# Moving the start of two loads in a decode attention kernel: x waits for GpSimd's last constant, the first K load waits for the x transposes

## The chip, the cores and the metric

The kernel runs on one core of one Trainium2 chip. The metric is the device time of one execution in microseconds (us). All runs quoted here are of one core. The kernel before repeats within 0.5 us.

## The reference

Two independent attention blocks, A and B, decode one token each for 8 sequences. Each has 32 heads of width 128 and a cache of 4096 keys and values per head, all in bf16.

```python
# for A and for B: x (8,1,1024), k_cache and v_cache (8,32,4096,128), wq (1024,4096), wo (4096,1024)
q = (x @ wq).reshape(B, Sq, H, Dh).transpose(0, 2, 1, 3)
scores = einsum("bhqd,bhkd->bhqk", q, k_cache) * (Dh ** -0.5)
p = softmax(scores, axis=-1)
o = einsum("bhqk,bhkd->bhqd", p, v_cache)
a = o.transpose(0, 2, 1, 3).reshape(B, Sq, H * Dh) @ wo
# result: concatenate([a, b], axis=-1)
```

The caches are large and each element is used once, so nearly all of the kernel's traffic is K and V: the profile counts 1107 MB read.

## The kernel before

All big loads go through a ring of three slots of 64 KB per partition, 8 MiB each. SyncE issues them in the order of a plan: A_wq, the first K load, B_wq, the second K load, then V and K in turns, last the two wo. Each load waits until the former tenant of its slot has been used. Two small loads (16 KB each) bring x to the third slot, which B_wq takes over once TensorE has transposed x.

```python
plan = [("wq", 0, 1), ("k", 0, 0), ("wq", 1, 2)]          # (what, which, slot)
for n in range(NQ - 1):
    plan.append(("k", n + 1, (n + 1) % 2))
    plan.append(("v", n, 2))
# ...
def load_tiles():
    while issued[0] < len(plan):
        kind, n, w = plan[issued[0]]
        prev = before[issued[0]]                              # former tenant of the slot
        dep = c_oh if (kind, n) == ("k", 0) else opUse.get(prev)
        if prev is not None and dep is None:
            return
        # ... dma(to, from_, ("t", w), [dep]) on SyncE

# GpSimd writes constants, one after another: ident, own_m, PM, E; c_E is the last of them.
c_oh = add("dve", lambda e: e.tensor_copy(own_h[:], own), [c_own])    # a VectorE constant

x_sb = ring[0:NC * B, 2, 0:D]
op_x = [dma(x_sb[c * B:(c + 1) * B, :], caches[c][0].rearrange("b s d -> b (s d)"), ("x", 0), [c_oh], "act") for c in range(NC)]
def emit_xT(e): ...                                           # 8 TensorE transposes of x
op_xT = opUse[("x", 0)] = add("pe", emit_xT, [c_ident, op_x[-1]])
load_tiles()
c_xT = add("dve", lambda e: e.tensor_copy(xT[:], misc_bf16[:, 0:NC * DC * B]), [op_xT])
make_q(0)                                                     # needs A_wq and xT
# ... make_qT, make_stage, make_qbc; then 64 steps of multiply, fold, reduce, softmax, PV
```

`add(engine, instruction, waits)` and `dma(out, in, semaphore, waits, engine)` record operations; a wait becomes a semaphore wait only where it is needed. A_wq has no wait and is issued first.

Of the kernel before, what the change touches and what calls it, by code (L numbers as in the profile page):

```python
# [31 lines left out]
class _Program:  # L32
# [11 lines left out]
    def add(self, eng, emit, deps=(), dma_key=None, moves=False):  # L44
        op = _Op(eng, emit, list(deps), dma_key, moves)
        if dma_key is not None:
            self.counts[dma_key] = self.counts.get(dma_key, 0) + 16
            op.token = (dma_key, self.counts[dma_key])
        for d in op.deps:
            if not (d.eng == "pe" and eng == "pe"):  # L50
                d.sig = True
        self.ops[eng].append(op)
        return op
# [86 lines left out]
def _build_kernel(nc, caches, out):  # L140
    B, Sq, D = caches[0][0].shape
    _, H, Sk, Dh = caches[0][1].shape
    NC = len(caches)
# [18 lines left out]
    with es:  # L162
# [44 lines left out]
        def dma(out_ap, in_ap, key, deps, eng="sp"):  # L207
            return add(eng, lambda e: e.dma_start(out_ap, in_ap), deps, dma_key=key)


        def pool_select(view, base, pattern, dep, op=ALU.not_equal, fill=1.0, step=1):
            return add("pool", lambda e: e.affine_select(out=view, in_=view, compare_op=op, fill=fill,
                                                         base=base, pattern=pattern, channel_multiplier=step), [dep])
# [9 lines left out]
        c_E = add("pool", lambda e: e.memset(E[:], 0.0))  # L223
        for q in range(4):
            c_E = pool_select(E[:, :, PH - 1:].rearrange("p i (j u) -> p i j u", u=PH)[:, :, :, 0], -32 * q, [[-8, 4], [-1, HQ]], c_E)
        c_oh = add("dve", lambda e: e.tensor_copy(own_h[:], own), [c_own])
# [5 lines left out]
        opOc, opNorm, opProj, opUse, opPM, opEv = {}, {}, {}, {}, {}, {}  # L232
# [16 lines left out]
        def where(n):  # L249

            return n // (B * HB), n // HB % B, n % HB
# [4 lines left out]
        def load_tiles():  # L256
            while issued[0] < len(plan):
                kind, n, w = plan[issued[0]]
                prev = before[issued[0]]
                dep = c_oh if (kind, n) == ("k", 0) else opUse.get(prev)  # L260
                if prev is not None and dep is None:
                    return
                to, key = ring[:, w, :], ("t", w)
                if kind in ("k", "v"):
                    c, b, hb = where(n)
                    from_ = caches[c][1 if kind == "k" else 2][b, hb * HQ:(hb + 1) * HQ].rearrange("u (m t) d -> (u m) (t d)", m=MP)
                    opT[(kind, n)] = dma(to, from_, key, [dep])
                elif kind == "wq":
                    opT[(kind, n)] = dma(to[:, 0:DC * H * Dh], caches[n][3].rearrange("(p k) n -> p (k n)", k=DC), key, [dep])
                else:  # L270
                    from_ = caches[n][4].rearrange("(p r) n -> p (r n)", r=H)
                    for i, (r0, r1) in enumerate(wo_cuts if n == NC - 1 else ((0, H),)):
                        opT[(kind, n, i)] = dma(to[:, r0 * D:r1 * D], from_[:, r0 * D:r1 * D], key if n < NC - 1 else ("w", i), [dep])
                issued[0] += 1
# [168 lines left out]


        x_sb = ring[0:NC * B, 2, 0:D]
        op_x = [dma(x_sb[c * B:(c + 1) * B, :], caches[c][0].rearrange("b s d -> b (s d)"), ("x", 0), [c_oh], "act") for c in range(NC)]

        def emit_xT(e):
            for k in range(DC):
# [2 lines left out]
            return i  # L452
# [3 lines that stand above are left out]
        make_q(0)  # L456
# [5 lines left out]
        for n in range(NQ):  # L462
            P.mark(n)
            for r in range(NR):
                s = n * NR + r
                make_mul(s)
                if s >= LAG:
                    make_red(s - LAG)
                if r == LAG - 1 and n >= 1:
                    make_shift(n - 1)  # L470
                fold = make_fold(s)
                if r == LAG - 1 and n >= 1:
                    make_pm(n - 1)
                if n == 0 and r == NR - 1:
                    for c in range(1, NC):
                        make_q(c)
                        make_qT(c)
                if r == 2 and n >= 1:
                    make_pv(n - 1, 0, RG // 2)
                if r == 3 and n >= 1:  # L480
                    make_pv(n - 1, RG // 2, RG)
                    make_acc(n - 1)
                if r == 2 and n + 1 < NQ:
                    make_stage(n + 1)
                    make_qbc(n + 1)
                make_eacc(s, fold)
                load_tiles()
                if r == 3 and n >= 1:
                    make_ext(n - 1)
        P.mark(NQ)  # L490
        n = NQ - 1
# [3 lines left out]
        make_pv(n, 0, RG)  # L495
        make_acc(n)
        load_tiles()
        make_ext(n)
        c_norm = make_norm()
# [34 lines left out]
def bass_concat_heads__mha_block_cached__mha_block_cached__decode_kernel(  # L534
    nc, A_x, A_k_cache, A_v_cache, A_wq, A_wo, B_x, B_k_cache, B_v_cache, B_wq, B_wo, out,
):
    caches = [(A_x, A_k_cache, A_v_cache, A_wq, A_wo), (B_x, B_k_cache, B_v_cache, B_wq, B_wo)]
    _build_kernel(nc, caches, out)
# [28 lines left out]
```

## Time and profile before

| | before |
|---|---|
| time, median of the first 3 runs | 2564.36 us (2564.36 to 2564.61) |
| span of the profiled execution | 2562.5 us |
| data read, mean rate | 1107 MB, 432 GB/s |
| VectorE busy | 85% |

These are lines of the page of the kernel before: its span, the rows of VectorE and of the DMA engines (busy tenths in 40 equal slices of the span), the DMA totals, and the costliest group of instructions (busy us, mean ns of one, then the engine's idle time just before them and what ended most of it).

```profile
span 2562.5 us, 18439 instructions
...
DVE  3798898898898898898898888988988988988983
...
DMA  9999999999999999999999999999999999999999
...
DMA packets 19545, 1107.49 MB, mean 432 GB/s; under 512 B 2208, under 2 KB 2240, under 8 KB 2384
...
L328 DVE TENSOR_TENSOR ring<-ring,qbc 128x8192 bf16<-128x8192 bf16 x256 | 1131.1, 4418 | 310.5 <-DMA ring<-in_A_k_cache_dram 157.3
```

The DMA row has no slice under 9. VectorE, the busiest engine of compute, still idles 310 us in all ahead of its first multiply of each K tile, and what ends that is a K load (A's 157 us, B's 153). So the DMA stream sets the pace. The single packet records say the same: a 64 KB packet takes 2.42 us on one of 16 engines, which is 65536 B x 16 / 2.42 us = 433 GB/s. This agrees with the Trainium skill, DMA: Bandwidth & Descriptors, section Where 436 GB/s comes from, which puts the ceiling of the 16 ports at 435 GB/s. Between the first data packet at 1.83 us and 2550 us the engines stand idle for 0.25 us each on average (16 minus the packets in flight, summed over time and divided by 16).

The start is the part that the change touches. This is the timeline of before there; the columns are start, duration, engine (SPq and ACTq are the queues that issue DMAs), line, operation, and in brackets how long the engine idled and what ended it.

```profile
0.80 0.40 SPq L208 DMA_DIRECT2D ring<-in_A_wq_dram  x1
...
4.20 0.35 SPq L208 DMA_DIRECT2D ring<-in_A_k_cache_dram  x1
4.21 0.59 ACTq L208 DMA_DIRECT2D ring<-in_A_x_dram  x1
...
4.30 1.49 POOL L212 TENSOR_SCALAR_AFFINE_SELECT E<-E 128x32 bf16<-128x32 bf16 x4
...
18.13 0.64 PE L450 MATMUL misc<-ident,ring 16*128 16x16 bf16 x8 [18.13 <-DMA ring<-in_B_x_dram]
18.80 0.33 SPq L208 DMA_DIRECT2D ring<-in_B_wq_dram  x1
...
22.95 3.59 PE L284 MATMUL o<-ring,xT 128*8 128x512 bf16 x32 [4.19 <-DMA ring<-in_A_wq_dram]
...
42.20 4.43 DVE L328 TENSOR_TENSOR ring<-ring,qbc 128x8192 bf16<-128x8192 bf16 x1 [8.50 <-DMA ring<-in_A_k_cache_dram]
```

A_wq, issued at 0.80, is at hand at 22.9. The first K load, issued at 4.20, is queued behind it and has landed at 42.2. The two small x loads, issued at 4.21 and 4.84, have both landed only at 18.0, because their packets take turns with those of A_wq. The packet records of one of the engines that serve x show it (start in us, duration in us, queue, bytes; q1 is SyncE's queue, q10 ScalarE's):

```
   7.221  2.420  q1   65536
   9.637  0.084  q10   2048     x of A
   9.717  2.418  q1   65536
  12.131  0.009  q10      4     its completion increment
  12.137  2.418  q1   65536
  14.551  0.084  q10   2048     x of B
  14.631  2.418  q1   65536
  17.045  0.009  q10      4     its completion increment
```

A note on clocks. The packet times in this document count from the same start as the timelines. The recorded texts below were written with packet times 0.30 us too late. The view by stretches shows it: data packets of A_wq (590 GB/s in the last column, where a packet counts at its start) start before 2.00 us already, where the recorded prediction has the first at 2.13:

```profile
1.00:2.00 1.00, 0.00 (x0) 0.00 (x0) 0.00 (x0) 0.00 (x0) 0.63 (x4) 1.00 1.74 590
```

So where a recorded text has a packet at 22.2, read 21.9, and where it takes 1.33 or 1.3 us from an issue to its first packet, read 1.03 (0.80 to 1.83). Each forecast of a turn or of a hole sets one packet time against another, so the error cancels there. Issue times, times of instructions and durations are not affected.

### The profile page before, as it was taken

The numbers are of one execution on the slowest core, as the hardware profiler recorded it, in microseconds if no ns is written. First come the engines' busy times: TensorE is split into PE (matmuls) and PEld (weight loads), VectorE is DVE, ScalarE is ACT, GpSimd is POOL, SyncE is SP. The second block draws the span as 40 slices with busy tenths as digits, with TensorE's granted clock in tenths as the row PEclk, the third lists the DMA queues.
The fourth block names the chain that finished last, engine by engine and source line by source line (L and its number), as shares of the span: only waits on it lengthen the run. The fifth ranks groups of instructions, "written<-read, shape, count | busy, mean of one in ns | idle before, by whom it ended". The sixth has DMA issues, their size and how long they took to land.

```text
span 2562.5 us, 18439 instructions
## 1 busy us (share of the span) xinstructions
PE 1120.6 (44%) x7520; PEld 391.4 (15%) x7520; DVE 2172.9 (85%) x1034; ACT 130.9 (5%) x403; POOL 4.3 (0%) x15
## 2 busy tenths in 40 slices
PE   2443443443444444434444444444444434434435
PEld 0111111111111111111111111111111111111112
DVE  3798898898898898898898888988988988988983
ACT  1100000000000000000000000000000000000000
POOL 0000000000000000000000000000000000000000
PEclk7676766766766666766666666767767676767677
DMA  9999999999999999999999999999999999999999
GB/s 425 427 438 430 437 431 437 431 437 431 437 431 437 431 437 431 437 431 435 432 436 430 436 431 437 431 435 433 432 436 432 435 431 437 431 436 432 436 432 394
DMA packets 19545, 1107.49 MB, mean 432 GB/s; under 512 B 2208, under 2 KB 2240, under 8 KB 2384
## 3 DMA queue, kind: packets, MB, share of 16 engines
q1 hardware_dynamic: 19472, 1107.32, 99.9%
q8 instruction: 6, 0.10, 0.0%
q10 hardware_dynamic: 64, 0.05, 0.0%
q14 instruction: 3, 0.02, 0.0%
HBM read 1107.33 MB, written 0.03 MB: 432 GB/s over the span
## 4 chain that ended last, share of the span: by engine, by line
DMA 51%; DVE 28%; issue 16%; PE 4%; another core or an unknown queue 0%; ACT 0%; DVEq 0%; SPq 0%; POOL 0%; POOLq 0%
DMA ring<-in_A_k_cache_dram 25%; DMA ring<-in_B_k_cache_dram 25%; DVE ring L328 10%; DVE ring L333 10%; PE red L343 4%; DVE s_sb L351 4%; DVE PM L368 3%; DMA ring<-in_B_wo_dram 2%; DVE rmax L357 1%; DVE rtmp L358 0%; ACT PM L290 0%; DVEq L135 0%; PE o L284 0%; DVE ngm L361 0%
## 5 line engine op out<-in xcount | busy, mean ns | idle before, releaser
L328 DVE TENSOR_TENSOR ring<-ring,qbc 128x8192 bf16<-128x8192 bf16 x256 | 1131.1, 4418 | 310.5 <-DMA ring<-in_A_k_cache_dram 157.3
L343 PE MATMUL red<-ring,ident 128*128 128x512 bf16 x2048 | 781.7, 551 | 1392.3 <-DVE ring L333 1392.3
L333 DVE TENSOR_TENSOR ring<-ring 128x4096 bf16<-128x4096 bf16 x256 | 581.4, 2271 | 0.0
L343 PEld LDWEIGHTS red<-ring,ident 128*128 128x128 bf16 x2048 | 238.9, 127 | 1843.5 <-DVE ring L333 1494.5
L351 DVE TENSOR_REDUCE s_sb<-red 128x64 f32<-128x1024 f32 x256 | 311.1, 1215 | 3.3 <-PE red L343 3.3
L380 PE MATMUL pv<-ring,PM 128*32 128x512 bf16 x4096 | 275.4, 416 | 4.7 <-DVE PM L368 4.7
L368 DVE TENSOR_TENSOR PM<-pe,own_h 128x2048 bf16<-128x2048 bf16 x64 | 146.1, 2284 | 0.7 <-ACT pe L363 0.7
L380 PEld LDWEIGHTS pv<-ring,PM 128*32 128x32 bf16 x4096 | 104.2, 104 | 189.3 <-issue 117.1
L317 ACT ACTIVATE qbc<-misc 128x128 bf16<-128x128 f32 x64 | 17.7, 277 | 1091.9 <-PE misc L315 1091.9
L363 ACT ACTIVATE pe<-s_sb,ngm 128x256 bf16<-128x256 f32 x64 | 32.5, 508 | 471.5 <-DVE ngm L361 471.5
L388 ACT ACTIVATE accS<-pv 128x512 bf16<-128x512 f32 x64 | 38.2, 597 | 351.8 <-PE pv L380 351.8
L397 PEld LDWEIGHTS o<-accS,E 128*32 128x32 bf16 x1024 | 31.3, 100 | 49.3 <-issue 48.1
L397 PE MATMUL o<-accS,E 128*32 128x32 bf16 x1024 | 38.1, 185 | 0.7 <-ACT accS L388 0.7
L403 ACT ACTIVATE o_sb<-o 32x32 f32 (+1 forms) x64 | 11.8, 185 | 449.7 <-PE o L397 449.7
L357 DVE TENSOR_REDUCE rmax<-s_sb 128x1 f32<-128x256 f32 x64 | 26.9, 420 | 2.2
L436 DVE CAST orow<-proj 8x512 bf16<-8x512 f32 x2 | 1.4, 679 | 24.6 <-PE proj L426 24.6
L426 PE MATMUL proj<-ring,on_sb 128*8 128x512 bf16 x128 | 16.4, 411 | 11.7 <-DMA ring<-in_A_wo_dram 8.0
L310 ACT ACTIVATE qst<-qT 128x128 bf16 (+1 forms) x64 | 18.7, 293 | 2.3 <-DVE qT L303 2.3
L358 DVE TENSOR_SCALAR rtmp<-half,rmax 128x32 f32<-128x32 f32 x64 | 15.4, 241 | 2.3
L303 DVE COPY qT<-misc 128x256 bf16<-128x256 bf16 x2 | 2.5, 1272 | 17.2 <-PE misc L299 17.2
L315 PE MATMUL misc<-ident,qst 128*128 128x128 bf16 x64 | 14.8, 232 | 1.7 <-ACT qst L310 1.7
L361 DVE TRANSPOSE_TENSOR_REDUCE ngm<-rtmp 128x1 f32<-128x32 f32 x64 | 13.5, 211 | 2.2
(34 smaller groups left out, 65.1 us busy)
## 6 DMA issues: line engine op xcount, KB each, us to landing
ring<-in_B_wo_dram SPq DMA_DIRECT2D x1, 4608.0 KB, 31.7
ring<-in_B_wo_dram SPq DMA_DIRECT2D x1, 2048.0 KB, 36.3
ring<-in_B_wo_dram SPq DMA_DIRECT2D x1, 1024.0 KB, 38.3
ring<-in_A_k_cache_dram SPq DMA_DIRECT2D x32, 39.8
ring<-in_A_v_cache_dram SPq DMA_DIRECT2D x32, 27.8
ring<-in_B_k_cache_dram SPq DMA_DIRECT2D x32, 40.0
ring<-in_B_v_cache_dram SPq DMA_DIRECT2D x32, 27.9
ring<-in_B_wo_dram SPq DMA_DIRECT2D x1, 512.0 KB, 39.1
```

Of the source, the lines that this page charges most:

```text
L310: return e.activation(qst[:, n % 2, :].rearrange("p (j m) -> p j m", m=MP), from_.unsqueeze(2).to_broadcast([128, HQ, MP]), ACTF.Copy)
L317: opQbc[n] = add("act", lambda e: e.activation(qbc[:, n % 2, :], misc[:, 0:Dh], ACTF.Copy), [opQb[n], _at(opMul, NR * (n - 2) + NR - 1)])
L328: opMul[s] = add("dve", lambda e: e.tensor_tensor(v, v, qbc[:, n % 2, :].unsqueeze(1).to_broadcast([128, CT, Dh]), ALU.mult), [opT[("k", n ...
L333: return add("dve", lambda e: e.tensor_tensor(v[:, :, 0:64], v[:, :, 0:64], v[:, :, 64:128], ALU.add), [opMul[s]])
L343: i = e.matmul(dst, ident[:], v[:, g, :, j, :], start=(j == 0), stop=(j == 3))
L351: opRed[s] = add("dve", lambda e: e.tensor_reduce(s_sb[:, n % 2, r * CT:(r + 1) * CT], red_ps[s % 2][:, :].rearrange("p (t w) -> p t w", w ...
L357: m = add("dve", lambda e: e.tensor_reduce(rmax[:], s_sb[:, n % 2, :], AX.X, ALU.max), [opRed[NR * n + NR - 1]])
L363: opExp[n] = add("act", lambda e, at: e.activation(pe[:], s_sb[:, n % 2, :], ACTF.Exp, bias=ngm[:, n % 2:n % 2 + 1], scale=scale, accum_ou ...
L368: opPM[n] = add("dve", lambda e: e.tensor_tensor(PM[:], pe[:].unsqueeze(2).to_broadcast([128, T, HQ]), own_h[:].unsqueeze(1).to_broadcast( ...
L380: i = e.matmul(pv_ps[32 * q:32 * (q + 1), :], PM[:, t:t + 4, :].rearrange("p t j -> p (t j)"), v[:, t * Dh:(t + 4) * Dh], start=(g == 0), ...
L388: opAcc[n] = add("act", lambda e: e.activation(accS[:], pv_ps[:], ACTF.Copy), [opPV[n], _at(opExt, n - 1)])
L397: x = e.matmul(to, E[:, i, PH - 1 - u:PH - 1 - u + MB], accS[:, i * 128 + H * u:i * 128 + H * (u + 1)], start=(i == 0 and u == 0), stop=(i ...
```

## The change

Its intent: the x loads and the first K load stay out of the way until A_wq's descriptors have been generated, so that the first weight load is generated alone. Only two waits change.

```diff
-                dep = c_oh if (kind, n) == ("k", 0) else opUse.get(prev)
+                dep = op_xT if (kind, n) == ("k", 0) else opUse.get(prev)
...
-        op_x = [dma(..., ("x", 0), [c_oh], "act") for c in range(NC)]
+        op_x = [dma(..., ("x", 0), [c_E], "act") for c in range(NC)]
```

The order of instructions on every engine stays the same.

More of the change, by code (lines that the diff above doesn't have):

```diff
@@ L445, in _build_kernel @@
         x_sb = ring[0:NC * B, 2, 0:D]
-        op_x = [dma(x_sb[c * B:(c + 1) * B, :], caches[c][0].rearrange("b s d -> b (s d)"), ("x", 0), [c_oh], "act") for c in range(NC)]
+        op_x = [dma(x_sb[c * B:(c + 1) * B, :], caches[c][0].rearrange("b s d -> b (s d)"), ("x", 0), [c_E], "act") for c in range(NC)]
         def emit_xT(e):
```

## The prediction

> **What bounds it.** The core's DMA engines. The page's DMA row reads 9 in all 40 slices and its byte line 1107 MB at 432 GB/s over 2562.5 us; VectorE is 85% busy and, by the groups, waits for K loads. The packet records of the trace agree: almost every packet is 64 KB, 2.42 us each; on 16 engines such packets alone take 2539 us. Their mean idle time between the first data packet (2.13 us) and 2550 us is 0.25 us. So only the 2.1 us before the first packet, a hole in the DMA stream, and the last 10 us can change the time.
>
> **What the change does.** Only waits move; instructions and their order stay. The first weight load (A_wq) is issued at 0.80 us as before. Timeline of before: the first K load is issued at 4.20, the x loads at 4.21 and 4.84, both released by VectorE's constant; the x packets land by 18, the transposes run 18.13 to 18.77, B_wq is issued at 18.80; A_wq has landed at 22.9, the first K load at 42.2.
> - The x loads now wait for GpSimd's last select (4.30 + 1.49 = 5.79): issued at about 5.8 instead of 4.2.
> - The first K load goes from 4.2 to about 18.8, right before B_wq, in the same order of the queue. A_wq occupies all 16 engines until about 22.2, so a K load issued at 18.8 still queues behind data.
>
> **What is critical.** The x loads are slow because each of their packets takes turns with a 64 KB packet of A_wq (first x packets at 9.94, then 12.4, 14.9, 17.3). This is the turn by turn arbitration per packet of the Trainium skill, DMA: Bandwidth & Descriptors, section Queues, rings and completion order; the trace's alternation agrees. From issue to first packet was 1.33 us for A_wq. An x load issued at 5.8 should be ready near 7.2, and the turns are taken near 7.5 to 8.1 for a start at 9.94, so it may still get the same turn (landing at 18, no hole), or miss one (2.42 us later: x at 20.5, the K load issued at 21.2, its first packet at 22.5 to 22.8 instead of 22.2).
> - Same turn (I give 55%): change 0, within 0.3 us.
> - One turn lost (40%): a hole of 0.4 to 0.7 us, plus a slow first wave as at the start (about 3.0 instead of 2.42 us per packet): +0.5 to +1.5 us, passed on whole, since nothing later has DMA slack to give it back.
> - Two lost: about +4 us.
>
> Gains: A_wq "alone" cannot land much earlier, since its packets already run at the 2.42 us of the steady stream; only its first wave shows an excess (0.6 us), and that began before K and x were issued.
>
> **Prediction.** 2564.9 us, range 2563.8 to 2566.6 (before: 2564.36). Faster by over 2%: 0.003; within 2%: 0.99; slower by over 2%: 0.007.
>
> **What would show it.** SyncE's second DMA issue moves from 4.2 to between 18.5 and 21.5 us and B_wq follows within 0.4 us; the x issue is at 5.8; x transposes at 18.1 (same turn) or near 20.5 (one lost); the first multiply, at 42.2 before, moves by exactly the hole (0 to 1.5 us); every later K landing and the end move by the same amount; DMA packets unchanged.
>
> **What would make it wrong.** x landing much later than 20.5, so that all engines stand still; the generation of the late K load's descriptors taking longer than the 1.33 us of A_wq; or A_wq gaining from the empty queue behind it.

## The result, and the profile after

The changed kernel took 2564.51 us (median of 6 runs, 2564.34 to 2565.04), the kernel before 2564.45 us (6 runs, 2564.36 to 2564.61). The ratio is 1.0001 with a 95% interval of 0.9988 to 1.0013: the same time. Ratios here are the mean time of one kernel's runs over that of the other's of the same rounds, so not quite the ratio of the medians. The range covers two of the forecast branches, so the number alone tests little; the issue times and turns below test more.

The timeline of the changed kernel, same stretch and columns:

```profile
0.80 0.40 SPq L208 DMA_DIRECT2D ring<-in_A_wq_dram  x1
...
5.83 0.59 ACTq L208 DMA_DIRECT2D ring<-in_A_x_dram  x1
...
18.19 0.65 PE L450 MATMUL misc<-ident,ring 16*128 16x16 bf16 x8 [18.19 <-DMA ring<-in_B_x_dram]
18.87 0.35 SPq L208 DMA_DIRECT2D ring<-in_A_k_cache_dram  x1
...
19.27 0.42 SPq L208 DMA_DIRECT2D ring<-in_B_wq_dram  x1
...
23.02 3.48 PE L284 MATMUL o<-ring,xT 128*8 128x512 bf16 x32 [4.19 <-DMA ring<-in_A_wq_dram]
...
42.27 4.42 DVE L328 TENSOR_TENSOR ring<-ring,qbc 128x8192 bf16<-128x8192 bf16 x1 [8.93 <-DMA ring<-in_A_k_cache_dram]
```

x is issued 1.62 us later and yet transposed at the same time. The first K load is issued 14.67 us later, and yet its data is multiplied only 0.07 us later. A_wq lands no earlier than before (23.02 against 22.95).

The chain of waits names this well. The first of these fences is before, the second after, each the long DMA piece of the chain at the start (start, duration, what):

```profile
4.20 37.98 DMA ring<-in_A_k_cache_dram
```

```profile
6.46 11.59 DMA ring<-in_B_x_dram
...
18.87 23.38 DMA ring<-in_A_k_cache_dram
```

Of the 37.98 us that the K load took from issue to landing before, 17.9 were spent in the queue behind A_wq, whose last packets end at 22.09 on average. Taking most of these away shortens "issue to landing" to 23.38 and brings no data earlier. A long time from issue to landing is not a cost where the engines are busy with earlier loads all the while.

The changed page's DMA row is 9 throughout again, and its span is 2562.6 us. That row alone can't rule out a hole: a slice is 64 us long. The packet records below do.

### The profile page after: what moved, and what is told of

Same layout as the page of the kernel before. It is cut to its first block, busy times and chain, and to the rows that moved or that the text cites. A ratio compares the mean times of both kernels' runs of the same rounds, so it can differ in the third digit from the quotient of the medians.

```text
span 2562.6 us, 18438 instructions
## 1 busy us (share of the span) xinstructions
PE 1121.8 (44%) x7520; PEld 391.5 (15%) x7520; DVE 2172.9 (85%) x1034; ACT 131.0 (5%) x403; POOL 4.3 (0%) x15
## 4 chain that ended last, share of the span: by engine, by line
DMA 51%; DVE 28%; issue 16%; PE 4%; another core or an unknown queue 0%; ACT 0%; POOL 0%; DVEq 0%; SPq 0%; ACTq 0%; POOLq 0%
DMA ring<-in_B_k_cache_dram 25%; DMA ring<-in_A_k_cache_dram 24%; DVE ring L328 10%; DVE ring L333 10%; PE red L343 4%; DVE s_sb L351 4%; DVE PM L368 3%; DMA ring<-in_B_wo_dram 2%; DVE rmax L357 1%; DMA ring<-in_B_x_dram 0%; DVE rtmp L358 0%; ACT PM L290 0%; DVEq L135 0%; DVE ngm L361 0%
```

## The experiments

Three theories were set against each other. *Slack*: the K load may be issued as late as one likes while A_wq keeps the engines busy; past that, each microsecond without data is added to the time whole. *Absorbing*: a late start is made good later, by VectorE's idle 15% for instance. *Cancelling*: one half of the change gains and the other loses as much.

For each run that moves all the bytes, three numbers were worked out from the packet records of its one profiled execution: the gap between the mean end of the last 16 packets of A_wq (one for each engine) and the mean start of the first 16 of K; the excess of those first 16 over 2.42 us; and the sum of both.

| run | K issued | gap | excess of first packets | sum | mean time against before |
|---|---|---|---|---|---|
| before | 4.20 | 0.00 | 0.00 | 0.00 | |
| x_only | 4.21 | 0.00 | 0.00 | 0.00 | +0.04 |
| x_first | 11.50 | 0.00 | 0.00 | 0.00 | +0.06 |
| k_only | 18.78 | 0.01 | 0.07 | 0.08 | +0.03 |
| changed kernel | 18.87 | 0.01 | 0.11 | 0.11 | +0.14 |
| x_late_a | 18.88 | 0.00 | 0.03 | 0.03 | -0.07 |
| x_late_b | 21.15 | 0.41 | 0.59 | 1.00 | +1.19 |
| x_late1 | 21.38 | 0.57 | 0.64 | 1.21 | +1.21 |
| k_after_wq | 23.13 | 2.13 | 0.72 | 2.85 | +2.77 |
| x_late2 | 23.70 | 2.77 | 0.74 | 3.51 | +3.53 |
| k_after_q | 26.70 | 5.82 | 0.59 | 6.42 | +6.59 |

All times are us. The last two columns agree within 0.2 us over the whole range. Differences under about 0.3 us are within the scatter of runs and are not claimed to be real. The rows come from several batches; each difference is against the runs of before of its own batch. The interval of each ratio is some 0.17% (4 us) wide to either side, so it excludes 1 only for k_after_q and the two half_wqB runs. The differences of 1.2 to 3.5 us rest on ranges of runs that do not overlap with those of before, and on the packets.

### x_only and k_only: each half of the change alone

```diff
 x_only:  - ("x", 0), [c_oh], "act"        + ("x", 0), [c_E], "act"
 k_only:  - dep = c_oh if (kind, n) == ("k", 0)   + dep = op_xT if (kind, n) == ("k", 0)
```

> Only the x loads wait for GpSimd's last constant (issue 5.8 instead of 4.2); the first K load stays at 4.2. Slack theory: the x packets get the same turns as before (first at about 10, last at 17.4 to 17.9), time within 0.5 us of before, 2564.4. Cancelling theory (a gain in one part hides a loss in the other): this part moves the time by over 0.5 us and the other part by as much the other way.

> Only the first K load waits for the transposes (issue about 18.8); x stays at 4.2. Slack theory: first K packets still start when the last packet of A_wq ends (22.2 to 22.7), no hole, time within 0.5 us of before. Cancelling theory: over 0.5 us away, opposite in sign to x_only.

Measured: x_only 2564.52 us (2564.45 to 2564.63), k_only 2564.49 us (2564.40 to 2564.69), before 2564.45. Neither half moves the time, so there is nothing that could cancel. That theory falls.

### k_after_wq: A_wq really alone in its queue

```diff
-                dep = op_xT if (kind, n) == ("k", 0) else opUse.get(prev)
+                dep = opT[("wq", 0)] if (kind, n) == ("k", 0) else opUse.get(prev)
```

> The first K load waits for A_wq to have landed, so that A_wq is really alone in its queue to the end. Slack theory: issue near 23.0, first packet 1.33 us later near 24.3, against 22.3: a hole of about 2.0 us, plus a slow first wave of about 0.6: time 2566.5 to 2567.5 (+2.0 to +3.0). If A_wq alone were worth something, A_wq would land visibly before 22.9. Absorbing theory (idle VectorE time takes up a late start): under +0.5.

Measured: 2567.16 us (2566.84 to 2567.89), +2.8 on the means. Its timeline:

```profile
23.13 0.35 SPq L208 DMA_DIRECT2D ring<-in_A_k_cache_dram  x1
...
23.25 3.22 PE L284 MATMUL o<-ring,xT 128*8 128x512 bf16 x32 [4.19 <-DMA ring<-in_A_wq_dram]
...
45.07 4.42 DVE L328 TENSOR_TENSOR ring<-ring,qbc 128x8192 bf16<-128x8192 bf16 x1 [11.77 <-DMA ring<-in_A_k_cache_dram]
```

Here nothing but x competes with A_wq from its first to its last byte, and it is still at hand no earlier than before (23.25 against 22.95). Being alone is worth nothing to it, since its packets run at the stream's 2.42 us anyway. The price is the hole. It shows in the view by stretches (stretch, its length, busy time of each engine, granted clock, DMA share, GB/s), first for the changed kernel, then for this one:

```profile
20.00:25.00 5.00, 1.98 (x20) 0.70 (x24) 0.00 (x0) 0.00 (x0) 0.00 (x0) 1.00 0.99 419
```

```profile
20.00:25.00 5.00, 1.75 (x20) 0.66 (x24) 0.00 (x0) 0.00 (x0) 0.00 (x0) 1.00 0.66 223
```

The DMA share falls from 0.99 to 0.66 in these 5 us. (A packet counts where it starts, so such shares are rough; the table above uses single packets.)

### k_after_q: the K load later still

```diff
-                dep = op_xT if (kind, n) == ("k", 0) else opUse.get(prev)
-                if prev is not None and dep is None:
+                dep = opQ.get((0, 0)) if (kind, n) == ("k", 0) else opUse.get(prev)
+                if (prev is not None or kind == "k") and dep is None:
                     return
...
         make_q(0)
+        load_tiles()
```

> The first K load waits for the first half of the q projection of A (issue near 26.4). Slack theory: first packet near 27.7, hole about 5.4 us plus 0.6: time 2569.8 to 2571.0 (+5.4 to +6.5), the first multiply moved by the same amount. Absorbing theory: under +1.

Measured: 2570.93 us (2570.86 to 2571.62), +6.6.

```profile
26.70 0.35 SPq L208 DMA_DIRECT2D ring<-in_A_k_cache_dram  x1
...
48.61 4.42 DVE L328 TENSOR_TENSOR ring<-ring,qbc 128x8192 bf16<-128x8192 bf16 x1 [14.77 <-DMA ring<-in_A_k_cache_dram]
```

The first multiply is 6.41 us later than before, the hole with its slow first packets 6.42, the end 6.6. None of it is given back in the 2520 us that follow, although VectorE has idle time in every step. The absorbing theory falls: idle time of VectorE did not bring bytes in faster. By itself this run would also fit a rival, a chain of compute that merely starts later; x_late_b and half_wqB_early speak against that.

### x_late1 and x_late2: x loses one turn, or two

A memset and 5 or 11 selects on a scratch tile, one after the other on GpSimd, hold the x loads longer; K still waits for the transposes. These bring about the two branches of the prediction that did not occur, one turn lost (40%) and two lost.

```diff
+        pad = sb("pad", [128, 32], BF16)
...
+        c_pad = add("pool", lambda e: e.memset(pad[:], 0.0), [c_E])
+        for q in range(5):                                 # 11 in x_late2
+            c_pad = pool_select(pad[:], -q, [[-1, 32]], c_pad)
...
-        op_x = [dma(..., ("x", 0), [c_E], "act") for c in range(NC)]
+        op_x = [dma(..., ("x", 0), [c_pad], "act") for c in range(NC)]
```

> The changed kernel with one memset and five selects on a scratch tile added on GpSimd ahead of the x loads: issue near 8.1. One turn lost: first x packet near 12.4, transposes near 20.5, K issue near 21.3, its first packet at 22.5 to 22.8 instead of 22.3. Slack theory: +0.3 to +1.3 us against before. Absorbing theory: 0.

> As x_late1 with eleven selects: x issue near 10.6. Two turns lost: transposes near 23, K issue near 23.7, first K packet near 25: hole about 2.7 us plus a slow first wave: +2.7 to +4.0 us by the slack theory; 0 by the absorbing theory. If some x packets find the engines with no A_wq packet left they go faster and the loss is smaller.

Measured: x_late1 2565.68 us (2565.28 to 2566.17), +1.2; x_late2 2568.02 us (2567.76 to 2568.29), +3.5. The selects took less time each than estimated, so x_late2 issued x at 9.91 instead of 10.6; it lost two turns as intended (first x packets from 14.40). Timeline of x_late1:

```profile
7.80 0.59 ACTq L209 DMA_DIRECT2D ring<-in_A_x_dram  x1
...
20.71 0.64 PE L454 MATMUL misc<-ident,ring 16*128 16x16 bf16 x8 [20.71 <-DMA ring<-in_B_x_dram]
21.38 0.35 SPq L209 DMA_DIRECT2D ring<-in_A_k_cache_dram  x1
```

### x_late_a and x_late_b: how near the changed kernel is to losing a turn

The same edit with no select (x_late_a) and with two (x_late_b).

> How far is the changed kernel from losing a turn? One memset on a scratch tile ahead of the x loads, issue near 6.05 instead of 5.83. Turn theory (an x packet must be queued, 1.3 us after its issue, before the engine starts the packet ahead of it at 7.5 to 8.0): queued near 7.35, still in time: x packets near 10, transposes near 18.2, time within 0.5 us of before. A fixed delay theory (x simply takes 12.4 us from issue to transposes): transposes near 18.4, the same time; the two part in x_late_b.

> The memset and two selects, issue near 6.8. Turn theory: queued near 8.1, after most engines started the packet ahead: most x packets near 12.4, transposes near 20.6, K issued near 21.3, +1.0 to +1.4 us as in x_late1, from a delay of only 1 us. Fixed delay theory: transposes near 19.2, K issued near 19.9, under +0.4.

Measured: x_late_a 2564.48 us (2564.21 to 2564.74), the same time; x_late_b 2565.73 us (2565.63 to 2565.83), +1.2. First x_late_a, then x_late_b:

```profile
6.00 0.59 ACTq L209 DMA_DIRECT2D ring<-in_A_x_dram  x1
...
18.22 0.64 PE L454 MATMUL misc<-ident,ring 16*128 16x16 bf16 x8 [18.22 <-DMA ring<-in_B_x_dram]
```

```profile
6.73 0.59 ACTq L209 DMA_DIRECT2D ring<-in_A_x_dram  x1
...
20.48 0.64 PE L454 MATMUL misc<-ident,ring 16*128 16x16 bf16 x8 [20.48 <-DMA ring<-in_B_x_dram]
21.15 0.35 SPq L209 DMA_DIRECT2D ring<-in_A_k_cache_dram  x1
...
44.55 4.42 DVE L332 TENSOR_TENSOR ring<-ring,qbc 128x8192 bf16<-128x8192 bf16 x1 [10.52 <-DMA ring<-in_A_k_cache_dram]
```

x landing goes in steps, not in proportion. Issued between 4.21 and 6.00 (nine of the runs), x is transposed at 18.1 to 18.4; issued at 6.73 or 7.80, at 20.5 to 20.7; issued at 9.91, at 23.0. A fixed delay is ruled out. Between 6.00 and 6.73 a turn is lost: in x_late_b seven of the eight x packets of A start at 12.1 to 12.3 and one still at 10.24. The changed kernel, at 5.83, therefore stands less than 0.9 us from a loss of 1.2 us; the kernel before stands nowhere near it, since its K load does not depend on x at all.

The last line of x_late_b shows a trap. Its first multiply is 2.35 us later than before, but its hole and slow first packets sum to 1.00 and its end is only 1.2 later (1.5 in the profiled execution). The first multiply waits for the slowest of the 16 engines: the last packets of the first K load end at 42.54 on average (41.43 before), on one engine at 44.20. So the prediction's "the first multiply moves by exactly the hole" does not hold here: the end stays nearer to the mean over the engines than to the first multiply.

### x_first: x with no wait at all

```diff
-        op_x = [dma(..., ("x", 0), [c_E], "act") for c in range(NC)]
+        op_x = [dma(..., ("x", 0), [], "act") for c in range(NC)]
```

> The changed kernel with the wait on the x loads taken away altogether (x has its own semaphore, and nothing else has written its rows of the ring): issued near 0.8 from ScalarE beside A_wq. x lands by 5 to 11 us, the transposes follow, K and B_wq are issued there instead of at 18.9. Slack theory: time within 0.5 us of before, since the stream has no hole in either; first packets of A_wq may start up to 0.3 us later or earlier and move the end by that.

Measured: 2564.56 us (2564.39 to 2564.73), the same time. x is issued at 0.80, transposed at 10.84, and K is issued at 11.50. The stream has no hole at K in the kernel before, in the changed kernel or in this one, and so the three take the same time. Among kernels in which K depends on x, this is the robust order, with the K load issued 10.6 us before A_wq's last packets end (mean); it is not faster.

### half_wqB and half_wqB_early: do bytes set the time?

half_wqB loads half of B_wq (4.19 MB less) and halves B's q projection. half_wqB_early also runs that projection one chunk earlier in the program.

```diff
-  opT[(kind, n)] = dma(to[:, 0:DC * H * Dh], caches[n][3].rearrange("(p k) n -> p (k n)", k=DC), key, [dep])
+  kk = DC // 2 if n else DC
+  opT[(kind, n)] = dma(to[:, 0:kk * H * Dh], caches[n][3].rearrange("(p k) n -> p (k n)", k=DC)[:, 0:kk * H * Dh], key, [dep])
 (make_q: k runs over kk = DC // 2 if c else DC, stop=(k == kk - 1))
 half_wqB_early, besides:
-                if n == 0 and r == NR - 1:
+                if n == 0 and r == NR - 2:
                     for c in range(1, NC): make_q(c); make_qT(c)
```

> Wrong result on purpose: the second weight load brings half of its bytes (4.19 MB less) and the projection of B uses half of the contraction. If the DMA stream's bytes set the time, it falls by 64 packets of 2.42 us over 16 engines: 9.7 us, to about 2554.8. If a pace of compute set it, it falls by less than 5.

Measured: 2556.55 us (2556.01 to 2557.54), -7.8 on the means and not the 9.7 expected. The comparison with the reference passed although q of B is wrong; its tolerance does not see this error, so the pass says nothing of the mathematics. The stretch 70 to 75 us shows where the rest went, first of the changed kernel, then of half_wqB, with the issue of the first V load there:

```profile
70.00:75.00 5.00, 1.74 (x30) 0.88 (x23) 2.02 (x1) 4.27 (x8) 0.00 (x0) 0.91 0.97 419
```

```profile
70.00:75.00 5.00, 1.48 (x21) 0.35 (x12) 2.64 (x2) 4.35 (x8) 0.00 (x0) 0.84 0.65 223
```

```profile
71.53 0.33 SPq L208 DMA_DIRECT2D ring<-in_A_v_cache_dram  x1
```

The first V load takes the slot of B_wq and waits for B's q projection. In the changed kernel it is issued at 71.29 and the engines have K data until 80.35 (mean). In half_wqB they run dry at 70.75, and the V packets start at 72.72 on average with 0.67 us of excess: a hole worth 2.64 us. In the profiled execution (2557.54 us, against 2564.34 for the changed kernel's) -9.7 + 2.6 gives -7.1, and -6.8 was measured; the other three runs were 0.6 to 1.5 us shorter, and were not profiled.

> half_wqB came out 7.9 us shorter instead of 9.7; its trace shows a new hole where the first V load, issued at 71.5 after the q projection of B, reaches the engines at 72.8 while they had run dry at 71.05. This kernel is half_wqB with the q projection of B moved one chunk earlier in the program (r = 2 of the first step instead of r = 3), so that the V load is issued near 64. Bytes theory with hole: no hole, time 2554.3 to 2555.3 (-9.7 within 0.5 us against before). If something other than that hole held the 1.8 us: stays near 2556.5.

Measured: 2555.24 us (2554.81 to 2555.57), -9.2. The V load is now issued at 63.23 and that hole is gone (the first V packets follow at once at 70.66, 2.42 us each). Of the 9.7 us, 9.2 arrive; 0.3 of the rest stands in the packets at the second V load, issued 2.2 us before the first engine would run dry (first packets 2.66 us instead of 2.42). So bytes set the time, as long as each load is issued early enough. It also speaks against a chain of compute that merely starts with the first multiply: that multiply starts at 42.25 here, as before, and the end comes 9.2 us earlier. (The run also drops matmuls, but TensorE was busy for only 44% of the time before.)

## Why the prediction was right

- **Bound by the DMA stream, only holes count.** Right. Each run with a hole came out longer by the hole, and taking 4.19 MB out took out 9.2 of 9.7 us.
- **x issued at 5.8, the same turn (55%).** Right: issue 5.83, transposes 18.19, K issue 18.87, B_wq 0.40 us after it. The estimate behind it, ready as long after the issue as A_wq's first packet (1.03 us by the timeline's clock) and served one 64 KB packet later, was tested by the four kernels that delay x and held: it puts the limit near 6.2 (7.24, the earliest turn, less 1.03), and the loss came between 6.00 and 6.73. At 55% against 40% the prediction did not claim to know this beforehand.
- **One turn lost: +0.5 to +1.5 us; two: about +4.** These branches did not come about in the changed kernel. Brought about on purpose, they cost 1.2 and 3.5 us, of which the gap was 0.41 to 0.57 in the first case and the slow first packets about 0.6. The second was put some 0.5 too high.
- **No gain for A_wq alone.** Right: at hand at 23.02 and, with K held off to the end, at 23.25, against 22.95 before.
- **The number.** 2564.9 was a mean over the branches; the branch that came about gave 2564.51, within the range of 2563.8 to 2566.6.

What stays open: in the changed kernel and in k_only, where K is issued some 3.1 us before the first of A_wq's last packets ends, part of the first K packets took up to 2.7 us, 0.1 us over 2.42 on average. The same shows in x_late_a (up to 2.63) and the half_wqB runs (up to 2.96), not where K is issued at 11.50 or earlier. Whether that reaches the time is below the scatter, and what delays those packets was not tried. The claim in the intent that descriptor generation is disturbed was tested only by its consequence, the landing of A_wq; generation itself is not visible in this profile.

No experiment points to a version that beats both kernels: with the bytes given and no hole in the stream, only the first 1.8 us and the last 10 us are left, and this change touches neither.

## What to carry to other kernels

In a kernel that its DMA stream bounds, a load's issue may be moved freely as long as the next load is queued before the engines run dry (issued some 3.1 us ahead was enough here); look for the share of the DMA engines in the stretch around it and for the packets there, not for the time from issue to landing. Holding a load back gives nothing to the load in front of it that already runs at full rate, and it turns a load that nothing gated into one that a small load's landing gates. A hole was paid in full here, and with it some 0.6 to 0.7 us for the first packets after it.

## What the Trainium skill lacked or had wrong

- DMA: Bandwidth & Descriptors, section Latency and other measured facts, gives about 600 ns to the first byte for loads issued by SyncE or ScalarE. Here the first data packet started 1.03 us after the issue of A_wq began, and 0.97 to 1.05 us after the issue of K loads that found the engines dry (k_after_wq, x_late2, k_after_q, x_late1). The packet record may not start where the page's first byte does; for planning an issue, the trace's 1.0 us counted.
- The same page, section Queues, rings and completion order, has each engine take turns between queues packet by packet, which the records confirm. It does not say what that costs a small load beside a large one: each turn was a 64 KB packet of 2.42 us, data and completion increment took a turn each, and the transposes that wait for two loads of 16 KB began 13.9 us after the first of their issues.
- No page has the lead that this needs: an x load had to be issued about 1.0 us and one more packet (3.5 us in all, an estimate from the 1.03 and 2.42 us above) before its turn. Issued at 6.00 it kept the turn near 9.9, at 6.73 seven of eight packets lost it.
- No page has the price of a restart: after a hole, the first packet on each engine took 3.0 to 3.2 us on average instead of 2.42, in six kernels, much as at the start of the kernel (2.9 to 3.2).
